# The value part of the row gradients, moved from the weight-gradient stage into the backward loop

## The chip, the cores and the metric

The kernel runs on one core of one Trainium2 chip. The metric is the device time in microseconds of one execution. A core has five engines that run side by side: TensorE (PE in the profile, with its weight loads as PEld), VectorE (DVE), ScalarE (ACT), GpSimd (POOL) and SyncE (SP). Each executes its own instructions in their order and waits on semaphores for the others. SP, ACT and POOL issue DMAs, which 16 DMA engines carry out. The DMAs that SP issues are the hardware queue q1 of the profile, POOL's are the software queue q0.

## The reference

The reference computes one forward pass and all its gradients (a vector-Jacobian product). Per 32-token segment, an attention over 8 memory rows and 32 token rows runs with 32 heads of 128 features, and its first 8 output rows are the next segment's memory; the result is gated by a feed-forward block:

```python
xn = layernorm(x)                       # 2048 tokens, 640 wide
for s in range(64):                     # segments
    h = concat([mem, xn[32*s:32*s+32]]) # 40 rows
    q, k, v = h @ Wq, h @ Wk, h @ Wv    # 32 heads of 128
    p = softmax(mask(q @ k.T * scale))
    o = (p @ v) @ Wo
    mem, out[s] = o[:8], o[8:]
g = silu(swiglu(xn, w1, w3, w2))
y = x + out * g
# outputs: y and the gradients of x, mem0, Wq, Wk, Wv, Wo, w1, w3, w2 for a given gradient of y
```

Backward, the segments run from the last to the first, because the gradient of a segment's memory rows is the gradient of the previous segment's outputs. For each row of h the gradient is the sum of three products: the gradients of v, k and q of that row (4096 wide each), times the transposed Wv, Wk and Wq. The gradient of v is P transposed times the gradient of o before Wo (here gO).

## The kernel before

The stages follow each other on one core: layer norm and the feed-forward pass, the forward recurrence, the backward loop (`phase4_Abwd`), the weight-gradient stage (`phase6_Awgrads`), the gradient of Wo (`phase6b_gWo`) and the backward feed-forward pass (`phase5_Bbwd_ln`). Within a stage, `in_order` fixes each engine's order to the one in which the program is written.

**The backward loop.** `chain(t, gap)` is one step, for segment t, from 63 down to 0. It multiplies the incoming gradient rows by the turned Wo (`packed_half`, L306: four groups of 32 columns of the array at once), turns the result to features (`packed_sel`, L314), forms the gradients of P and of the scores for the 8 memory rows (L1226, L1236 to L1244, `bd`, `gkv` at L1195), and adds up the gradient of the memory rows in one PSUM bank with `packed_out` (L325). `packed_out` takes 64 matmuls for each of Wv, Wk and Wq; each has 8 columns (the memory rows) in a group of 32, so 24 columns of each group are unused. L1262 forms the gradients of the 8 queries from the key rows `kr`. `fold_add` (L334, L336) adds the bank's halves on ACT and DVE, `fold_turn` (L352) turns the sum to features, and L1283 puts it into the input of step t-1. So each step starts when `fold_turn` of the step before has ended.

Between these parts, `gap` puts the work on the ordinary rows: units of three segments and four heads (`ld`, `turn`, `dprob`, `dsoft`, `gmem`), two or three units a step, for t from 62 to 4. In the gap G4 one more product on PE (L1430, `WARM`) writes a bank that nobody reads.

**Loads.** For step t-1, `loads` (VTD, PM, QM: L1151, L1153, L1156), `load_k` (L1162, L1167) and `load_xp` (L1174) are issued by SP in the middle of step t, together with the unit loads (L1307, L265, L1311), two stores of dS (L1273) and the store of the step's gO rows (L1215). The key rows have two buffers, `krbs`, which alternate from step to step; so have Qst and Pm.

**The weight-gradient stage.** It runs eight passes (qd), each over 22 units of four heads. Per unit: `s1` turns dS (L1588), `s2` forms the gradients of v, k and q for the unit's rows (L1598), `s3` turns these to features (L1630) into `ring`, and `s4` multiplies them by Wv, Wk and Wq and adds to `acc` (L1648, 12 matmuls for 128 rows and half of the width). At the end of a pass, `wg` forms four heads of the three weight gradients (L1667). `Fetch` issues the unit loads five units ahead on SP and POOL. The finished row gradients go to GXA.

Of the kernel before, what the change touches and what calls it, by code (L numbers as in the profile page):

```python
# [9 lines left out]
BF16 = mybir.dt.bfloat16  # L10
# [6 lines left out]
P = 128  # L17
# [23 lines left out]
class K:  # L41
# [109 lines left out]
    def setup_dram(self):  # L151
# [15 lines left out]
        self.GXA = mk("GXA", (S, D))  # L167
        self.HRO = mk("HRO", (self.NR, D))
# [93 lines left out]

    def load_x(self, dst, off, srcs, eng):
        for (a, b, src) in srcs:
            eng.dma_start(dst[off + a:off + b], src)  # L265
# [64 lines left out]
def fold_add(k, pm, pool, tag="fup"):  # L330

    fs = pool.tile([64, 320], BF16, name="fsum", tag="fsum")
    up = pool.tile([64, 320], F32, name="fup", tag=tag)
    k.nc.scalar.copy(up[:], pm[64:128, 0:320])  # L334
    for c in (0, 160):
        k.nc.vector.tensor_tensor(fs[:, c:c + 160], pm[0:64, c:c + 160], up[:, c:c + 160], ALU.add)  # L336
    return fs


def fold_store(eng, dst, fs):  # L340

    for b in range(2):
        eng.dma_start(dst[:, 320 * b:320 * b + 320], fs[32 * b:32 * b + 8, :])
# [211 lines left out]
def recurrence(k, W0, W4, Wv, Wk_, Wq, Wo, own, ps, banks):  # L555
    nc, tc = k.nc, k.tc
    D, DC, S, H, HD, T = k.D, k.DC, k.S, k.H, k.HD, k.T
    with tc.tile_pool(name="achain", bufs=1) as ch, \
# [39 lines left out]
        def chain(t, gap):  # L598
# [96 lines left out]
            fs = fold_add(k, pm, ch)  # L695
# [387 lines left out]
def phase4_Abwd(k, out2, W0, W4, WT, own, ps, banks):  # L1083
# [20 lines left out]
    with tc.tile_pool(name="gst", bufs=1) as st, tc.tile_pool(name="gchain", bufs=1) as ch, \  # L1104
# [10 lines left out]
        Qsts = [two(k0[:, c:c + 256]) for c in (3072, 3328)]  # L1115
# [4 lines left out]
        krbs = [st.tile([120, 2048], BF16, name="krb")[:], vt[0:120]]  # L1120
# [9 lines left out]
        WARM = dict(G4=1)  # L1130
# [16 lines left out]
        def loads(t):  # L1147
# [4 lines left out]
            Pm = ch.tile([P, 2, 40], BF16, name="gPm", tag="gPm", bufs=2)  # L1152
            nc.sync.dma_start(Pm[:], k.PM[t].rearrange("p (a c) -> p a c", a=2))  # L1153
            Qst = Qsts[t % 2]
            for a in range(2):
                nc.sync.dma_start(Qst[:, a, :], k.QM[t, :, a * 2048:(a + 1) * 2048])  # L1156
            ins[t] = vT, Pm, Qst

        def load_k(t):
            kr = krbs[t % 2][0:104]  # L1160
# [23 lines left out]
        def chain(t, gap):  # L1184
# [3 lines left out]
            vT, Pm, Qst = ins.pop(t)  # L1188
            xp = xps.pop(t)
            bdP, bdS = bds  # L1190
            bd(nc.gpsimd, bdP, Pm)
            def gkv(i, lh, rh):
                pk = bB[:, 256 * i:256 * i + 256].rearrange("p (a c) -> p a c", a=2)
                for a in range(2):
                    nc.tensor.matmul(pk[:, a, :], lh[:, a, :], rh[:, a].rearrange("p h m -> p (h m)"), start=True, stop=True)  # L1195
                g_ = ch.tile([P, H, 8], BF16, name="gkv", tag=f"gkv{i}")
                nc.vector.scalar_tensor_tensor(g_[:].rearrange("p (u h) m -> p u (h m)", h=4),  # L1197
                                               pk.rearrange("p a (u c) -> p (a u) c", c=32), k.scale if i == 0 else 1.0,
                                               xp[:, :, i, :], op0=ALU.mult, op1=ALU.add)
                return g_  # L1200

            sg = ch.tile([P, 1024], BF16, name="gstg", tag="gstg", bufs=1)
# [8 lines left out]
            gmT = ch.tile([P, 2, 8, 16], BF16, name="gmT", tag="gmT")  # L1211
# [3 lines left out]
            nc.sync.dma_start(k.GOS[t // 4, :, :, t % 4].rearrange("g r c -> (g r) c"), sg[:])  # L1215
            gap("W1")
            gOst = ch.tile([P, 2, P], BF16, name="gOst", tag="gOst")
# [3 lines left out]
            nc.vector.tensor_copy(gOst[:], pgo[:])  # L1221
# [6 lines left out]
            gvT = gkv(1, gOst, bdP)  # L1228
            dprob_m(1)
            dPT = ch.tile([40, 2, P], BF16, name="dPT", tag="dPT")  # L1230
            nc.scalar.copy(dPT[:], psd.rearrange("p a q h -> p a (q h)"))
            gap("G1")
            packed_out(k, pm, gvT, WvT, True, False, 0, 5)
# [3 lines left out]
            pr = ch.tile([P, 2, 40], F32, name="gpr", tag="gpr")  # L1237
            nc.vector.tensor_tensor(pr[:], ps2[:], Pm[:], ALU.mult)
            Dm = ch.tile([P, 2], F32, name="Dm", tag="Dm")
            nc.vector.tensor_reduce(Dm[:], pr[:], axis=AX.X, op=ALU.add)  # L1240
            u = ch.tile([P, 2, 40], F32, name="gu", tag="gpr")
            nc.vector.tensor_tensor(u[:], ps2[:], bc_last(Dm[:], 40), ALU.subtract)
            dS = ch.tile([P, 2, 40], BF16, name="dSm", tag="dSm", bufs=2)
            nc.vector.tensor_tensor(dS[:], u[:], Pm[:], ALU.mult)  # L1244
# [3 lines left out]
            packed_out(k, pm, gvT, WvT, False, False, 5, 16)  # L1248
            gkT = gkv(0, Qst, bdS)
            ps3 = bview(bC, 104, 1, P, bf=True)[:, 0]  # L1250
            for a in range(2):
                nc.tensor.transpose(ps3[64 * a:64 * a + 40, :], dS[:, a, :], k.ident[:], tile_position=(0, 64 * a))
            dST = ch.tile([104, 8, 16], BF16, name="dSTm", tag="dPT")
# [10 lines left out]
            gqT = ch.tile([P, H, 8], BF16, name="gqT", tag="gqT")  # L1264
            for a in range(2):
                nc.scalar.activation(gqT[:, 16 * a:16 * a + 16, :], pgq[a], ACT.Copy, scale=k.scale)
            if t > 0:
                load_k(t - 1)
                ride(t - 1)
            with nc.allow_non_contiguous_dma(reason="mem rows of dS"):  # L1270
# [7 lines left out]
            fs = fold_add(k, pm, ch, "gstg")  # L1278
            gap("G4")
            if t > 0:  # L1280
                pt = fold_turn(k, bC, fs)
                gap("G5")
                nc.vector.tensor_copy(goxs[(t - 1) % 2][:, :, 0:8], pt[:])  # L1283
            fold_store(nc.gpsimd, k.m_rows(k.GWO, t - 1) if t > 0 else out2f, fs)
            gap("G6")

# [71 lines left out]
        def gmem(tl, qd):  # L1358
# [8 lines left out]
            ks = fl.tile([P, ns, 2, 4, 8], F32, name="gks", tag="gks", bufs=2)  # L1367
# [25 lines left out]
        def gap_of(t):  # L1393
# [5 lines left out]
            def gap(g):  # L1399
# [19 lines left out]
                elif g == "G5":  # L1419
                    at(gmem_ld, t, 1)  # L1420
                elif g == "G6":
                    at(dsoft, t, 2)
                if t == 0 and g == "G1":
# [26 lines left out]
        def gx_work():  # L1450
# [5 lines left out]
            for i, (x0, w) in enumerate(blocks):  # L1456
                for cg in range(4):
                    sg = ch.tile([P, 1024], BF16, name="gstg", tag="gstg", bufs=1)[:] if cg % 2 == 0 else xs2
                    for b in range(2):
                        gx_block(k, gx[:, i % 2], sg, (bA, bB)[b], WoT, x0, w, cg, b, nc.scalar)  # L1460
# [12 lines left out]
        for i in range(len(pro) + 2):  # L1473
# [15 lines left out]
            if i == len(pro):  # L1489
                for _ in work:  # L1490
                    pass
                loads(T - 1)
                load_xp(T - 1)
# [5 lines left out]
        assert not later  # L1499
        in_order(k, start)  # L1500
# [3 lines left out]
class Fetch:  # L1504

    def __init__(self, k, W0):
# [4 lines left out]
        t = W0.tile([P, 5 * self.NB * 512 + 12 * k.D], BF16, name="land", tag="w0")  # L1511
# [5 lines left out]
        self.ws = [four(t[:, c + 4 * k.D * i:c + 4 * k.D * (i + 1)]) for i in range(3)]  # L1517
# [774 lines left out]
```

## Time and profile before

| | us |
|---|---|
| median of three runs (lowest, highest) | 4712.01 (4704.07, 4719.22) |
| the profiled execution's own time | 4684.61 |
| its span, first to last instruction | 4682.7 |
| PE busy, share of the span | 4466.5 (95%) |
| DVE, ACT, POOL busy | 2244.7, 1587.4, 2098.4 |
| forward stages and turn to backward | 0 to 1826 |
| backward loop, from the second step on | 1826 to about 2898 |
| weight-gradient stage | about 2900 to 4115 |
| gradient of Wo, backward feed-forward | 4115 to 4682.7 |

A row of a timeline gives start, length, engine, line, operation, output and input names, and a count where equal instructions follow each other; a bracket at its end names the idle time before it and what ended it. `x40` with 2.34 us means that 40 matmuls together took 2.34 us, pipelined: the single one's length is more than the distance to the next. Names of buffers are those of the tile they are cut from: `kT` holds many small buffers of the loop, `gor`, `vt` and `krb` are row buffers.

### The profile page before, as it was taken

Reading aid. Unit: us, or ns where it says so; the run is one execution under the profiler, and the core shown is the slowest. Engines: PE = TensorE matmul, PEld = TensorE weight load, DVE = VectorE, ACT = ScalarE, POOL = GpSimd, SP = SyncE. Lnnn points to the kernel's source line nnn. Section 1 sums busy time; section 2 is a strip of 40 time slices with the busy share of each in tenths; the row PEclk is TensorE's granted clock in tenths of the full one; section 3 lists DMA queues with packets and bytes.
Section 4 is the critical chain, followed back from the end, with each engine's and each line's share of the span. In section 5 each row is a group of like instructions: output and inputs, shape, how many; then the busy total and the mean of one; then the engine's idle time right before and its main releaser. Section 6 shows DMA issues by size and latency. Waiting matters only on the chain. (4 is left out here: it accounts for less than half of the span.)

```text
span 4682.7 us, 159785 instructions
## 1 busy us (share of the span) xinstructions
PE 4466.5 (95%) x64504; PEld 2821.1 (60%) x64504; DVE 2244.7 (48%) x7156; ACT 1587.4 (34%) x4360; POOL 2098.4 (45%) x3528
## 2 busy tenths in 40 slices
PE   8999999999999898999999998999999999999999
PEld 4544555555555555666666665676667666666675
DVE  8734666666666534555555553343224432311460
ACT  5432555555544433333333332232223322200000
POOL 6532555555555423455444444354335533311440
PEclk9999999999999998999999999999999999999999
DMA  8773566666655677777777775664345543579783
GB/s 269 236 252 119 175 178 178 179 179 179 180 168 167 167 181 230 211 225 207 215 211 209 208 209 154 144 163 132 110 116 158 147 129 107 170 223 207 159 181 100
DMA packets 976843, 834.77 MB, mean 178 GB/s; under 512 B 518890, under 2 KB 858286, under 8 KB 974144
## 3 DMA queue, kind: packets, MB, share of 16 engines
q1 hardware_dynamic: 763879, 547.92, 42.2%
q0 software_dynamic: 129952, 228.13, 16.4%
q10 hardware_dynamic: 82275, 48.52, 4.0%
q8 instruction: 509, 8.34, 0.8%
q14 instruction: 228, 1.87, 0.1%
HBM read 472.66 MB, written 310.33 MB: 167 GB/s over the span
## 5 line engine op out<-in xcount | busy, mean ns | idle before, releaser
L1667 PE MATMUL wg<-gr,hr 128*128 128x512 bf16 x2400 | 521.7, 379 | 0.0
L1648 PE MATMUL g<-land,ghacc 128*128 128x320 bf16 x3072 | 459.9, 300 | 0.8
L1667 PEld LDWEIGHTS <-hr 128*128 128x128 bf16 x2400 | 233.9, 98 | 278.9
L306 PEld LDWEIGHTS <-hx 128*32 128x32 bf16 x10240 | 246.8, 96 | 229.1 <-issue 14.6
L1648 PEld LDWEIGHTS <-ghacc 128*128 128x128 bf16 x3072 | 289.2, 98 | 104.2 <-ACT ghacc L92 2.2
L90 DVE CAST wgo<-wg 128x512 bf16<-128x512 f32 x72 | 49.8, 692 | 471.2 <-PE wg L1667 471.2
L90 DVE CAST stg<-bank 128x512 bf16<-128x512 f32 x256 | 177.1, 692 | 158.6 <-PE bank L306 154.5
L880 POOL DMA_DIRECT2D OR<-xv x163 | 89.8, 551 | 361.1 <-ACT xv L92 338.5
L1613 POOL DMA_DIRECT2D GSP<-grs x48 | 25.5, 542 | 473.1 <-ACT grs L1605 472.0
L92 ACT COPY ghacc<-t6g 128x768 bf16<-128x768 bf16 (+1 forms) x176 | 137.1, 779 | 293.8 <-PE t6g L1630 284.5
L1324 POOL DMA_DIRECT2D VTD<-gvT x176 | 129.4, 742 | 218.7 <-ACT gvT L1323 209.5
L325 PEld LDWEIGHTS <-gkv 128*8 128x8 bf16 x8192 | 177.6, 86 | 82.2 <-issue 4.1
L832 POOL TENSOR_TENSOR xP<-xP,xrz 120x480 bf16<-120x480 bf16 x163 | 161.1, 988 | 76.0 <-DVE xrz L831 46.6
L812 ACT ACTIVATE xP<-xsp,xnm 120x120 bf16<-120x120 f32 (+1 forms) x540 | 186.1, 372 | 26.0 <-DVE xnm L794 25.9
L1654 DVE TENSOR_TENSOR ghacc<-ghacc,g 128x320 f32<-128x320 f32 x192 | 93.6, 487 | 209.9 <-PE g L1648 209.9
L336 DVE TENSOR_TENSOR fsum<-bank,fup 64x160 bf16<-64x160 f32 x254 | 69.5, 311 | 258.5 <-ACT fup L334 255.2
L92 ACT CAST wgo<-wg 128x512 bf16<-128x512 f32 x48 | 28.1, 585 | 479.8 <-PE wg L1667 407.0
L1371 POOL DMA_DIRECT2D GXP<-gks x157 | 91.0, 580 | 189.5 <-ACT gks L1369 188.8
L325 PE MATMUL bank<-Wo,oTm 128*32 128x320 bf16 x4032 | 154.2, 307 | 18.4 <-DVE oTm L684 18.4
L325 PE MATMUL bank<-WkT,gkv 128*8 128x320 bf16 x4096 | 162.8, 299 | 4.2 <-issue 2.2
L325 PE MATMUL bank<-WvT,gkv 128*8 128x320 bf16 x4096 | 166.4, 305 | 0.5 <-DVE gkv L1197 0.5
L306 PE MATMUL bank<-Wq,hx 128*32 128x512 bf16 x2560 | 161.6, 381 | 0.0
(389 smaller groups left out, 10916.1 us busy)
## 6 DMA issues: line engine op xcount, KB each, us to landing
QVS<-stg SPq DMA_DIRECT2D x128, 256.0 KB
kT<-VTD SPq DMA_DIRECT2D x64, 320.0 KB
PR<-xP POOLq DMA_DIRECT2D x168, 120.0 KB, 3.1
VTD<-gvT POOLq DMA_DIRECT2D x168, 120.0 KB, 4.0
land<-DSR SPq DMA_DIRECT2D x168, 120.0 KB
land<-PR SPq DMA_DIRECT2D x168, 120.0 KB
OR<-xv POOLq DMA_DIRECT2D x163, 120.0 KB, 3.0
orr<-OR SPq DMA_DIRECT2D x14, 1280.0 KB
```

Source lines behind the costliest of these rows:

```text
L90: return nc.vector.tensor_copy(out, in_)
L92: return nc.scalar.copy(out, in_)
L306: k.nc.tensor.matmul(bank[32 * g:32 * g + 32, :], x[:, dc, :], W[:, dc, c0:c0 + 512], start=(dc == 0), stop=(dc == k.DC - 1), tile_positio ...
L325: k.nc.tensor.matmul(pm[p0:p0 + nq, 0:320], x[:, h, :], W[:, h, 320 * b:320 * b + 320], start=(first and i == 0), stop=(last and i == 15), ...
L812: nc.scalar.activation(Pb[0:n, j, 0:n], sp[0:n, j, :], ACT.Exp, bias=nmx[0:n, j:j + 1], scale=k.scale, accum_out=Z[0:n, j:j + 1])
L832: eng.tensor_tensor(Pb[0:n, :, 0:n], Pb[0:n, :, 0:n], bc_last(rz[0:n], n), ALU.mult)
L880: q.dma_start(k.OR[120 * tl:120 * tl + n, c0:c0 + 512], v[0:n])
L1324: nc.gpsimd.dma_start(k.VTD[tl][:, :, h0:h0 + 4, :], vTq[:])
L1371: (nc.sync if (tl, qd) in pro else nc.gpsimd).dma_start(k.GXP[tl, :, qd, 0:ns], ks[:].rearrange("p s i h m -> p s i (h m)"))
L1648: nc.tensor.matmul(pg[:], ring[:, i, j, r0:r0 + P], Ws[qd][i][:, j, 320 * h:320 * h + 320], start=(i == 0 and j == 0), stop=(i == 2 and j ...
L1654: nc.vector.tensor_tensor(a, a, pg[:], ALU.add)
L1667: nc.tensor.matmul(pw[:], hr[:, tl, dc * P:(dc + 1) * P], grs[i][:, tl, :], start=(tl == 0), stop=(tl == NF - 1))
```

## The change

The value part of the row gradients is computed in the backward loop, and the weight-gradient stage computes the key and query parts alone.

- The stationary operand of the value product in `packed_out` becomes `gv`, with 32 columns per head: columns 0 to 7 are the memory rows of segment t as before, columns 8 to 31 are the value gradients of 24 of the 32 token rows of segment t+1, formed in the step before. The matmuls stay 64.
- `ride_v` forms them: 32 products of 40 rows (gO rows `rows`, probabilities `prc`), which `load_g` brings with eight DMAs on SP. `ride_copies` moves them into `gv` and, for the remaining 8 rows, into `lv`. Each fourth step `extra` multiplies `lv` by the turned Wv (64 matmuls in the gap G3). `last_v` does what is left after step 0.
- The results go to the new DRAM tensors GXV (through `fold_store`) and GXL, which `extra_rows` copies into GXV.
- `load_g(t)` stands after `load_k(t-1)` and ahead of the dS stores; `ride_v(t)` stands between the gap G4 and `fold_turn`. One of the two row buffers holds `rows`; `kr` is always the other. Qst, Pm, dS and gks have one buffer; several small tiles share the tag `seq`; `sg`, `prc` and `up` share one tile. `load_q` is split from `loads` and stands after `gkv(0)`. The mask product for P is moved from the step's start to the end of the step before. `WARM` is empty.
- In the weight-gradient stage, `s3` turns two parts (one copy on ACT, one on DVE), `s4` has 8 matmuls, and in the first pass `acc` starts from GXV rows that `gv_ld` loads on POOL. The value weights are no longer loaded. `s2` still forms the value gradients' rows, which `wg` needs.

```diff
@@ phase4_Abwd
-        Qsts = [two(k0[:, c:c + 256]) for c in (3072, 3328)]
+        Qst = two(k0[:, 3072:3328])
+        Pm, dS = [two(k0[:, c:c + 80]) for c in (3584, 3664)]
-        krbs = [st.tile([120, 2048], BF16, name="krb")[:], vt[0:120]]
+        rows = st.tile([120, 2048], BF16, name="gor")[:]
+        krbs = [rows, vt[0:120]]
+        gs = st.tile([P, 1152], BF16, name="gs")
+        sg, prc = gs[:, 0:1024], gs[0:104, 640:1152].rearrange("p (h c) -> p h c", c=32)
+        lv = st.tile([P, H, 32], BF16, name="lv")
+        gv = st.tile([P, H, 32], BF16, name="gv")
-        WARM = dict(G4=1)
+        WARM = {}
+        def load_q(t):
+            for a in range(2):
+                nc.sync.dma_start(Qst[:, a, :], k.QM[t, :, a * 2048:(a + 1) * 2048])
+        def load_g(t):
+            tl, s = t // 3, t % 3
+            nx = k.geo(tl)[2]
+            for a in range(2):
+                r = rows[64 * a:64 * a + 40]
+                nc.sync.dma_start(r[0:8].rearrange("r (g c) -> r g c", g=2),
+                                  k.GOS[t // 4, 2 * a:2 * a + 2, 0:8, t % 4, :].rearrange("g r c -> r g c"))
+                src = k.g_rows(t, a)
+                nc.sync.dma_start(r[8:40].rearrange("r (g c) -> r g c", g=2) if len(src.shape) == 3 else r[8:40], src)
+                for (p0, p1, r0) in ((0, 8, nx + 8 * s), (8, 40, 32 * s)):
+                    nc.sync.dma_start(prc[64 * a + p0:64 * a + p1],
+                                      k.PR[tl][r0:r0 + p1 - p0, 16 * a:16 * a + 16, 32 * s:32 * s + 32])
+        def ride_v(t):
+            pvs = [ps.tile([P, 16, 32], F32, name="rpv", tag="x", bufs=5) for _ in range(2)]
+            for j in range(16):
+                for a in range(2):
+                    p0 = 64 * a
+                    nc.tensor.matmul(pvs[a][:, j, :], rows[p0:p0 + 40, j * P:(j + 1) * P], prc[p0:p0 + 40, j, :],
+                                     start=True, stop=True, tile_position=(p0, 0))
+            return pvs
+        def ride_copies(t, pvs):
+            for a in range(2):
+                nc.scalar.copy(gv[:, 16 * a:16 * a + 16, 8:32], pvs[a][:, :, 0:24])
+                nc.scalar.copy(lv[:, 16 * a:16 * a + 16, 8 * (t % 4):8 * (t % 4) + 8], pvs[a][:, :, 24:32])
+        def extra(m, bank):
+            packed_out(k, bank, lv, WvT, True, True)
+            fs = fold_add(k, bank, lf[:, 0:640].bitcast(F32), lf[:, 640:960])
+            for b in range(2):
+                nc.gpsimd.dma_start(k.GXL[32 * m:32 * m + 32, 320 * b:320 * b + 320], fs[32 * b:32 * b + 32, :])
+        def extra_rows(m0, m1):
+            nc.gpsimd.dma_start(k.GXV[:, :].rearrange("(t r) d -> t r d", r=32)[4 * m0:4 * m1, 24:32],
+                                k.GXL[:, :].rearrange("(t r) d -> t r d", r=8)[4 * m0:4 * m1])
-            kr = krbs[t % 2][0:104]
+            kr = krbs[1][0:104]
@@ chain
-            packed_out(k, pm, gvT, WvT, True, False, 0, 5)
+            packed_out(k, pm, gv, WvT, True, False, 0, 5)
             if t > 0:
                 load_k(t - 1)
                 ride(t - 1)
+            load_g(t)
             gap("G4")
+            pvs = ride_v(t)
             if t > 0:
                 pt = fold_turn(k, bC, fs)
+                bd(nc.gpsimd, bdP, Pm)
                 gap("G5")
                 nc.vector.tensor_copy(goxs[(t - 1) % 2][:, :, 0:8], pt[:])
+            ride_copies(t, pvs)
             fold_store(nc.gpsimd, k.m_rows(k.GWO, t - 1) if t > 0 else out2f, fs)
+            if t + 1 < T:
+                fold_store(nc.gpsimd, k.GXV[32 * t + 32:32 * t + 56, :], fs, 8)
+        def last_v():
+            packed_out(k, pm, gv, WvT, True, True)
+            fs = fold_add(k, pm, up, ch.tile([64, 320], BF16, name="fsum", tag="fsum"))
+            fold_store(nc.gpsimd, k.GXV[0:24, :], fs, 8)
+            extra(0, bB)
+            extra_rows(0, 1)
-            ks = fl.tile([P, ns, 2, 4, 8], F32, name="gks", tag="gks", bufs=2)
+            ks = fl.tile([P, ns, 2, 4, 8], F32, name="gks", tag="gks")
+                if g == "G3" and t % 4 == 3 and t < T - 1:
+                    extra((t + 1) // 4, ps.tile([P, 512], F32, name="exb", tag="x", bufs=5))
+                if g == "G5" and t == 1:
+                    extra_rows(1, T // 4)
@@ phase6_Awgrads
-        def s3(u, i0, i1):
+        def s3(u):
+            for i in range(2):
+                pt = pa.tile([P, 4, nx], BF16, name="t6g", tag=bank("x", 5, 3))
+                gr = st.pop(("g", u, i + 1))
+                k.copy(ring[:, i, :, a:a + nx], pt[:], eng='sv'[i])
+        def gv_ld(p):
+            for (w, r0, h) in parts[p] if p < NTL else ():
+                if h == 0:
+                    gvs[w] = io.tile([P, D], BF16, name="gxv", tag="gxv", bufs=4)
+                    nc.gpsimd.dma_start(gvs[w][:], k.GXV[P * w:P * w + P, :])
-            for i in range(3):
+            for i in range(2):
                 for j in range(4):
                     nc.tensor.matmul(pg[:], ring[:, i, j, r0:r0 + P], Ws[qd][i][:, j, 320 * h:320 * h + 320],
             if qd == 0:
-                nc.vector.tensor_copy(a, pg[:])
+                nc.vector.tensor_tensor(a, gvs[w][:, 320 * h:320 * h + 320], pg[:], ALU.add)
```

## The prediction

> **What bounds the kernel now.** I read the page first: PE busy 95%, PEclk almost everywhere 9. A busy share is an average over stages, so next came the busy times of the stages the change touches: the backward loop, the first pass of the weight-gradient stage, and the rest of that stage.
>
> ```profile
> 1826.00:2882.00 1056.00, 1008.08 (x23674) 661.91 (x23678) 553.56 (x2814) 346.07 (x1157) 502.84 (x914) 1.00 0.71 204
> 2900.00:3000.00 100.00, 89.12 (x984) 70.61 (x984) 44.50 (x101) 39.40 (x65) 68.60 (x124) 0.91 0.87 209
> 3000.00:4115.00 1115.00, 1108.99 (x9407) 713.03 (x9406) 366.62 (x787) 306.53 (x510) 471.01 (x846) 1.00 0.48 132
> ```
>
> Columns: stretch, length, busy time of PE, PEld, DVE, ACT, POOL, PE clock, DMA share, GB/s. The loop (about 63 steps of 17.0 us) has PE at 95%, but the DMA engines are busy 0.71 as well. After 3000 us PE is busy 99.5%: what is taken from PE there is time. The first pass has DMA at 0.87 (1.0 from 2920 to 2960 in 20 us windows) and PE at 89%: data bound it.
>
> Then one step of the loop, in order of time, on PE (start, length):
>
> ```profile
> 2424.86 2.34 PE L306 MATMUL bank<-WoT,hx 128*32 128x512 bf16 x40
> ...
> 2434.95 0.59 PE L1262 MATMUL bank<-dSTm,vt 40*128 40x8 bf16 x32
> ...
> 2437.50 2.35 PE L325 MATMUL bank<-WqT,gqT 128*8 128x320 bf16 x64
> ...
> 2440.06 0.38 PE L1430 MATMUL bank<-WqT,ident 128*128 128x512 bf16 x1
> 2440.72 0.78 PE L352 MATMUL bank<-sel,fsum 64*128 64x8 bf16 x6 [0.29 <-DVE fsum L336]
> ...
> 2441.89 2.34 PE L306 MATMUL bank<-WoT,hx 128*32 128x512 bf16 x40
> ```
>
> Counted from the step's start: query products (L1262) end at +10.7, query part of the output starts at +12.6 (64 matmuls, 2.3 us), the warm-up product at +15.2, the fold's turn (L352) at +15.9, the next step at +17.0. The same step on SP, which issues its DMAs in written order:
>
> ```profile
> 2432.28 1.33 SPq L1156 DMA_DIRECT2D kT<-QM  x2
> 2433.66 0.47 SPq L1162 DMA_DIRECT2D krb<-KS  x1
> 2434.18 0.33 SPq L1167 DMA_DIRECT2D krb<-KS  x1
> 2434.55 0.32 SPq L1162 DMA_DIRECT2D krb<-KS  x1
> 2434.92 0.53 SPq L1167 DMA_DIRECT2D krb<-KS  x1
> 2435.56 1.25 SPq L1273 DMA_DIRECT2D DSR<-dSm  x2
> 2437.11 0.57 SPq L1174 DMA_DIRECT2D xp<-GXP  x1
> ```
>
> The four key loads take 1.9 us and start at +8.8, before L1262 ends: they fill the other of two buffers. Issuing costs 0.3 to 0.65 us a piece. By lines and medians SP spends about 11 us of 17 on it (with 0.07 us between issues, 13).
>
> Last, the stage where work goes away:
>
> ```profile
> 3097.35 1.79 PE L1648 MATMUL g<-land,ghacc 128*128 128x320 bf16 x12
> 3098.98 0.34 PE L1630 MATMUL t6g<-ident,gr 96*128 96x96 bf16 x4
> 3099.15 0.61 PE L1598 MATMUL r6p<-land 120*128 120x128 bf16 x8
> ```
>
> Start to start, 12 products of L1648 take 1.63 us (0.136 each), four transposes of L1630 0.17 us (0.042 each).
>
> **What the Trainium skill says.** "TensorE: Matmul & The Clock Gate", Part 3: matmuls on separate column groups run together, so a group's unused columns cost nothing. The trace agrees: 64 packed products with 8 columns take 2.35 us (0.037 each). Part 1 there: after a window of 3.4 us with too little work PE runs at half clock. The trace agrees: between 2900 and 2910 us PE is busy 4.17 us and the clock is 0.54. "DMA: Bandwidth & Descriptors", Anatomy of one DMA: about 2.0 us fixed from issue to semaphore; the small DSR stores from POOL land in 1.8 to 5.7 us, median 3.1. Same page, Issuing engines are not separate DMA queues: issue time is "usually small relative to the DMA itself"; in this loop the trace says otherwise.
>
> **Part 1, taken from the weight-gradient stage.** One third of 3072 products: 1024 x 0.136 = 139 us. One third of the 2112 transposes: 704 x 0.042 = 30 us. Together 169 us, 21 per pass of eight. The first pass is bound by data and gains 16 loads of 160 KB (2.6 MB, 12 us at 217 GB/s) for 0.65 MB of weights saved: I take 0 there (bounds +10 to -10). In the other seven, loads must come faster; the unit part of a pass now moves data at 0.81 to 0.98 share in its first 30 us, so I leave 2 to 3 us a pass to waits: 7 x 18.6 = 130 us gained (90 to 150). The copies shrink (ACT 798 ns for 768 columns becomes a 384-column one like DVE's 354) and stay beside PE.
>
> **Part 2, added products in the loop.** The packed value product now carries 24 row columns in the same 64 instructions: 0, by the price above. The extra product for the last rows: 64 x 0.037 = 2.34 us in every fourth step. The 32 row products (40 rows, 32 columns) are like L1262: 0.53 us a step. The warm-up product goes: 0.22 us a step. On PE alone: 15 x 2.34 + 63 x 0.3 = 54 us, less what falls into the 0.3 to 0.9 us that PE waits for fsum: about 40. ACT gets four copies (about 1.5 us a step on an engine busy 33%), POOL two more stores (1.06 us, busy 48%): both hidden beside PE; without that cover 1.5 and 1.1 us a step. The moved mask product on POOL only needs Pm, loaded 8 us earlier. Buffers that become single (gks, Pm, dS, the scratch tag) are reused no sooner than their readers end in the chain's own order; gks must see its store land (3.7 us) within 4.2, which would cost ACT up to 1 us ahead of the gstg copy if the step kept its length.
>
> **Part 3, added loads, on the path.** One row buffer now holds gradient rows, so the key rows have a single buffer: load_k must wait for L1262 (+10.7) instead of starting at +8.8. Behind it in SP's order stand eight new loads, and the row products wait for all eight. They stand in PE's order ahead of the fold's turn, behind which waits the whole next step.
>
> - load_k: +10.7 to +12.6.
> - load_g: two memory-row loads (like L1162, 0.79 together), two row loads (0.33 each, median of L1167), four loads of probabilities in 64-byte pieces, priced like DSR (0.62 each), eight gaps of 0.07: 0.79 + 0.67 + 2.5 + 0.5 = 4.5. Last issue starts at +16.4.
> - Landing 2.0 us later (bounds 1.8 and 3.1): +18.4. Row products 0.55, then turn to next step 1.17: +20.1 instead of +17.0, so 3.1 us a step, x 63 = 195 us. The 40 us of part 2 vanish in this wait.
> - On SP the DSR stores, GXP and the next unit loads stand behind load_g and start 4.5 us later or more. GXP is then issued at about +18.5, lands by +20.5, and is needed 4.5 us into the next step, so it does not set the end; a unit's rows loaded there are needed 3 us into the next step, about when they land.
> - PE then idles from +15.2 to +18.4. That nearly fills a clock window, except in the 15 steps with the extra product. In 48 steps I add 0.9 us for work at half clock: 43 us. No row shows it; bounds 0 and 1.7 (a whole window lost).
> - SP's total becomes 13 + 4.5 = 17.5 of 20 us; I add 0.1 us a step, 7 us.
>
> Sum for the loop: +245 us (bounds +70 and +390: every issue at 0.3 and landing 1.8, or landing 3.1 with issues of 0.9 for the 512-piece loads and a full window lost). DMA engines have room: 1280 pieces and 160 rows of 2 KB add to a share of 0.71, spread over a longer step.
>
> **Part 4, the seam.** At step 0 the eight loads stand behind the prefetch of the next stage; then two packed products, two folds and three dependent stores before the first unit: +10 us (5 to 15), partly in PE's wait of 5.8 us at 2902.
>
> Sum: +245 - 130 + 10 = +125 us. From the profiled 4684.6 us that is 4810; the runs' median lies 27 above the profile, so 4712 + 125 = 4837.
>
> **The rivals.**
>
> - A (0.58): as above, 4837; its own range 4750 to 4940.
> - B (0.18), ends below 4698: the loads come in time. Priced: with every issue at 0.3 (lowest seen 0.27 to 0.32) load_k and load_g take 4.4 us, the last starts at +14.8, lands at +16.6; the step grows by 1.3 us, 82 us in all: 4712 + 82 + 10 - 130 = 4674. It decides at (130 - 10) / 63 = 1.9 us a step, an average issue of 0.43 us with its gap, against the 0.52 that I sum. For it: plain two-dimensional loads (xP<-PR) take 0.38. Against: every row with three-dimensional pieces (QM, GXP, DSR) takes 0.57 to 0.63.
> - C (0.14): SP or the 64-byte pieces become the bound, and unit loads come late too: a step of 22.7 us, 5.7 x 63 - 120 = +240, 4950. For it: SP's load above, and steps of 18.3 to 19.8 us that occur already near 2233 and 2251. Against: median steps keep to 17.03.
> - D (0.10): A, and the weight-gradient stage is held by its loads and keeps half the gain: 4900.
>
> **How the numbers follow.** Within 0.3% (4698 to 4726) can't be told from no change. Faster: B and a little of A, 0.18; same 0.05; slower 0.77. The range goes to 4670, B's working, and 4975, past C, leaving out the tails of both.
>
> **What would show it.** Right: the first row product waits for a DMA onto gor or gs, some 3 us a step; steps near 20 to 21 us; PE clock below 1 in the loop; the key loads on SP start only after L1262's counterpart; L1648's counterpart has 2048 products, the stage is about 130 us shorter, its first pass unchanged. Wrong: row products that follow at once, steps under 19 us, or a stage that shortens by 70 or by 170.

## The result and the profile after

The changed kernel takes 4964.1 us (median of four runs, 4955.4 to 4970.9), the kernel before 4708.0 in runs beside it (4695.1 to 4719.2). The ratio is 1.054, with an interval of 1.051 to 1.058: slower by 5.4%. The profiled execution has a span of 4953.6 us where the kernel before has 4682.7.

The 271 us between the two spans, by the starts of the loop's feature copy (L1276, before L1221, once a step) and of the weight products (L1751, before L1667):

| piece | before | after | difference |
|---|---|---|---|
| start to the first step's copy | 1810.5 | 1824.1 | +13.6 |
| 63 steps of the loop | 1075.7 | 1387.1 | +311.4 |
| last step, seam, first pass up to its weight products | 113.3 | 127.6 | +14.3 |
| from there to the start of the last weight product | 1113.2 | 1043.8 | -69.4 |
| the rest | 570.0 | 571.0 | +1.0 |

Stretches of the changed kernel, which answer to the three that the prediction shows: the loop, seam with first pass, and the rest of the weight-gradient stage. Columns as there: stretch, length, busy time of PE, PEld, DVE, ACT, POOL, PE clock, DMA share, GB/s.

```profile
1826.00:3205.00 1379.00, 1166.51 (x26858) 763.89 (x26861) 568.06 (x2855) 423.93 (x1429) 589.17 (x1077) 0.89 0.66 179
3205.00:3340.00 135.00, 103.88 (x1264) 75.51 (x1257) 48.79 (x121) 38.38 (x80) 92.87 (x166) 0.82 0.76 193
3340.00:4384.00 1044.00, 982.68 (x7884) 605.33 (x7883) 364.55 (x786) 262.36 (x510) 472.50 (x847) 0.99 0.53 137
```

PE is busy 85% of the loop instead of 95%, at a clock of 0.89. The last stage has PE at 94%, where it had 99.5%: it no longer bounds that stage alone. A step of the loop on PE (start, length; a bracket names idle time and what ended it):

```profile
2415.34 3.94 PE L314 MATMUL bank<-WoT,hx 128*32 128x512 bf16 x40
...
2427.04 0.58 PE L1318 MATMUL bank<-dSTm,vt 40*128 40x8 bf16 x32
...
2429.58 2.35 PE L333 MATMUL bank<-WqT,gqT 128*8 128x320 bf16 x64
2434.64 0.17 PE L1194 MATMUL rpv<-gs,gor 40*128 40x32 bf16 x1 [2.33 <-DMA DSR<-kT]
2435.72 0.59 PE L1194 MATMUL rpv<-gs,gor 40*128 40x32 bf16 x31 [0.91 <-DMA gs<-PR]
2436.15 0.62 PE L358 MATMUL bank<-sel,fsum 64*128 64x8 bf16 x6
```

PE waits ahead of the row products (L1194) in two pieces. The store named in the first bracket is the event that ended last by the profile; the row products read `gs` and `gor` alone. After such a wait the clock is low: the step shown follows a wait of 4.7 us, and its first 40 products, by Wo, take 3.94 us instead of 2.34, at a granted clock of 0.59; those of the next step take 4.46 us at 0.50. The median over the 64 steps is 3.99 us. So the query products (L1318) end 12.3 us after the step's start instead of 10.7. The same step on SP's queue:

```profile
2424.89 0.32 SPq L1169 DMA_DIRECT2D kT<-PM  x1
...
2427.65 0.30 SPq L1216 DMA_DIRECT2D vt<-KS  x1
...
2429.43 0.33 SPq L1181 DMA_DIRECT2D gor<-GOS  x1
...
2431.67 1.80 SPq L1186 DMA_DIRECT2D gs<-PR  x2
2433.51 1.24 SPq L1330 DMA_DIRECT2D DSR<-kT  x2
```

The key loads start at +12.3, when L1318 ends; the eight new loads follow at +14.1; the last are out at +18.1. The page's group of the row products gives their whole idle time on PE:

```profile
L1194 PE MATMUL rpv<-gs,gor 40*128 40x32 bf16 x2048 | 47.8, 178 | 196.8 <-DMA gs<-PR 161.5
```

196.8 us over 64 steps is 3.1 us a step.

### The profile page after: what moved, and what is told of

It reads as the page before. It is cut to its first block, busy times and chain, and to the rows that moved or that the text cites. A ratio compares the mean times of both kernels' runs of the same rounds, so it can differ in the third digit from the quotient of the medians.

```text
span 4953.6 us, 163919 instructions
## 1 busy us (share of the span) xinstructions
PE 4489.7 (91%) x65848; PEld 2805.6 (57%) x65848; DVE 2254.3 (46%) x7190; ACT 1616.1 (33%) x4633; POOL 2198.5 (44%) x3707
## 3 DMA queue, kind: packets, MB, share of 16 engines
q14 instruction: 240, 1.97, 0.1%
## 5 line engine op out<-in xcount | busy, mean ns | idle before, releaser
L1751 PE MATMUL wg<-gr,hr 128*128 128x512 bf16 x2400 | 521.7, 379 | 0.1
L314 PEld LDWEIGHTS <-hx 128*32 128x32 bf16 x10240 | 272.1, 105 | 286.0 <-issue 105.2
L1751 PEld LDWEIGHTS <-hr 128*128 128x128 bf16 x2400 | 233.9, 98 | 279.1 <-issue 0.3
L1730 PE MATMUL g<-land,ghacc 128*128 128x320 bf16 x2048 | 329.8, 307 | 1.9 <-DVE ghacc L1734 1.7
L314 PE MATMUL bank<-WoT,hx 128*32 128x512 bf16 x2560 | 248.7, 564 | 5.1 <-DVE hx L1342 1.2
L1730 PEld LDWEIGHTS <-ghacc 128*128 128x128 bf16 x2048 | 195.0, 100 | 68.9 <-issue 2.2
L1194 PE MATMUL rpv<-gs,gor 40*128 40x32 bf16 x2048 | 47.8, 178 | 196.8 <-DMA gs<-PR 161.5
L1438 ACT ACTIVATE gks<-gkp 128x96 f32<-128x96 f32 (+1 forms) x352 | 71.4, 264 | 392.6 <-PE gkp L1435 352.2
L819 ACT ACTIVATE xP<-xsp,xnm 120x120 bf16<-120x120 f32 (+1 forms) x540 | 186.6, 374 | 25.7 <-DVE xnm L801 25.6
L1673 PE MATMUL r6p<-land 120*128 120x128 bf16 (+1 forms) x1408 | 122.9, 225 | 63.9 <-DMA land<-QVS 22.9
L333 PE MATMUL bank<-WvT,gv 128*32 128x320 bf16 x4160 | 174.4, 312 | 1.4 <-ACT gv L1200 0.8
L92 ACT COPY ghacc<-t6g 128x384 bf16<-128x384 bf16 (+1 forms) x176 | 82.6, 469 | 266.8 <-PE t6g L1706 264.0
L333 PE MATMUL bank<-WkT,kT 128*8 128x320 bf16 x4096 | 162.2, 299 | 2.6 <-DVE kT L1253 1.8
```

Of the source, the lines that this page charges most:

```text
L92: return nc.scalar.copy(out, in_)
L314: k.nc.tensor.matmul(bank[32 * g:32 * g + 32, :], x[:, dc, :], W[:, dc, c0:c0 + 512], start=(dc == 0), stop=(dc == k.DC - 1), tile_positio ...
L333: k.nc.tensor.matmul(pm[p0:p0 + nq, 0:320], x[:, h, :], W[:, h, 320 * b:320 * b + 320], start=(first and i == 0), stop=(last and i == 15), ...
L819: nc.scalar.activation(Pb[0:n, j, 0:n], sp[0:n, j, :], ACT.Exp, bias=nmx[0:n, j:j + 1], scale=k.scale, accum_out=Z[0:n, j:j + 1])
L1673: nc.tensor.matmul(pr[:, j * P:(j + 1) * P], lh[0:n, j, :], rw[i][0:n, j * P:(j + 1) * P], start=True, stop=True)
L1730: nc.tensor.matmul(pg[:], ring[:, i, j, r0:r0 + P], Ws[qd][i][:, j, 320 * h:320 * h + 320], start=(i == 0 and j == 0), stop=(i == 1 and j ...
```

## The experiments

The step is the distance of the first and the last copy of L1276 (or its counterpart), divided by 63: 17.07 us before, 22.02 after. Steps and totals of experiments are of one run each, against 4694 to 4714 for the kernel before beside them; the four runs of the changed kernel spread over 15.6 us.

**First: is it the loads' place, the loads, or the products?**

The loads early:

```diff
                 loads(t - 1)
+            load_g(t)
             packed_out(k, pm, gv, WvT, False, False, 5, 16)
...
-            load_g(t)
```

> The eight loads of load_g are issued ahead of load_q and load_k instead of behind them; nothing else differs from the changed kernel. Theory (the place in SP's order is the cost): the row products find their data and follow at once, PE no longer idles, the clock stays full; a step is 17.1 us plus 0.5 for the extra products and 0.1, so 17.7 instead of 22.0, and the kernel takes 4964 - 63 x 4.3 = about 4690 us. Rival (SP's total issue time or the DMA engines set the step): the order does not matter, steps stay above 20 us and the kernel above 4840.

Measured: 4840.2 us, step 20.26. The rival holds. The place is worth 1.76 us of the 4.95 that a step grew.

The row loads left out (the x-gradient's value part is not computed; the products stay and work on what lies in their buffers):

```diff
+        nc.gpsimd.memset(gs[:], 0.0)
...
-            load_g(t)
```

> load_g is left out; the row products work on what lies in their buffers (cleared once), so the gradient of x is not computed rightly. The loop keeps all products, copies and stores. Theory: a step of 17.6 us, the kernel at about 4685 us, within 20 us of the run with the loads issued early. Rival (the loads cost by their traffic and issue time wherever they stand): this kernel is faster than the one with early loads by more than 60 us, 1 us a step.

Measured: 4726.7 us, step 18.29. So all of the change in the loop except the loads (products, copies, stores, single buffers) costs 1.22 us a step, against some 0.5 expected, and the loads 3.73. The loads still cost 1.97 a step in the early place. The clause on the difference to the early placement decides as well: it is 113 us, more than 60, so the loads cost wherever they stand. The stretch from 2000 to 2800 us, early loads above, no row loads below, shows how:

```profile
2000.00:2800.00 800.00, 722.30 (x16834) 479.82 (x16827) 363.73 (x1852) 274.70 (x922) 383.32 (x702) 0.92 0.74 200
2000.00:2800.00 800.00, 760.20 (x18892) 519.51 (x18884) 406.35 (x2073) 304.84 (x1034) 428.81 (x784) 0.99 0.72 202
```

By the length of a step, PE is busy 18.3 us and idle 2.0 with the early loads, 17.4 and 0.9 without. The products are the same, so some 0.9 of the 1.97 us is work at the lower clock of 0.92, and the rest is idle time of PE. Early loads do not leave the clock whole.

Only the four probability loads left out, from the late place (the x-gradient's value part is not computed; `gs` is cleared once here too):

```diff
-                for (p0, p1, r0) in ((0, 8, nx + 8 * s), (8, 40, 32 * s)):
-                    nc.sync.dma_start(prc[64 * a + p0:64 * a + p1],
-                                      k.PR[tl][r0:r0 + p1 - p0, 16 * a:16 * a + 16, 32 * s:32 * s + 32])
```

> Of load_g's eight loads only the four of probabilities (64-byte pieces) are left out, so the gradient of x is not computed rightly; the four loads of gradient rows stay in their place. Theory (issues stand in line): four issues of about 0.65 us fall away, a step is 22.0 - 2.6 - 0.3 = 19.1 us, the kernel at about 4780 us. Rival (64-byte pieces are slow to land): more than the issue time is saved, a step under 18.2 us and the kernel under 4730.

Measured: 4838.3 us, step 20.30. Neither number: half of the eight loads is 1.72 us, about half of what all eight cost.

Fourteen warm-up products of 512 columns in the gap before the row products:

```diff
-        WARM = {}
+        WARM = dict(G4=14)
```

> The changed kernel with 14 warm-up products (0.22 us each, 3.0 us) in the gap G4, ahead of the row products, where PE waits for the loads. Theory (a part of the longer step is PE at half clock after the wait): the query products end at +10.9 instead of +12.3, the step is about 20.7 us, the clock in the loop above 0.97, the kernel at about 4885 us. Rival (the clock does not matter, the loads' time is fixed otherwise): the step stays at 21.8 to 22.2 us or grows.

Measured: 4897.7 us, step 21.15, query products ending at +10.7 again; the clock between 2000 and 2800 us is 0.99 where the changed kernel has 0.90. The theory holds, with a smaller gain than its 20.7 us: the warm-up gives back 0.87 us a step, 55 us.

**Second: what do the loads cost when they are early?** The early placement left 20.26 us. Three candidates: that they are waited for, that 1280 pieces of 64 bytes load the DMA engines, or SP's queue itself.

The loads where the early placement has them, without row products and copies (the x-gradient's value part is left out):

```diff
-            pvs = ride_v(t)
...
-            ride_copies(t, pvs)
```

> The early placement with its eight loads a step, but no row products and no copies of them: nobody waits for the loads (the x-gradient's value part is left out). The products alone, without the loads, cost 1.2 us a step (18.3 against 17.1). Theory, the loads cost what they put on the queue and on the DMA engines, waited for or not: step 18.8 us or more, total 4750 or more. Rival, what costs is the row products' wait for their landing: step 17.6 or less, total 4675 or less.

Measured: 4874.9 us. One line's view of the copy, from its first to its last start:

```profile
L1277 DVE COPY kT<-bank x64: 290/291/293, 1827.2 to 3117.7; 128x256 bf16<-128x256 bf16 x64
```

(3117.7 - 1827.2) / 63 = 20.48 us a step: the theory. Loads that nobody waits for cost as much as loads that are waited for, and the row products and their copies add nothing beside them. The wait for their landing is not needed for the cost. What waits instead is seen in the view of waits, 2000 to 2800 us (total, times, longest):

```profile
PEld L1388 <- issue: 40.9, 16, 7.0
PE gvpt L1388 <- DMA kT<-QVS: 37.8, 14, 7.0
```

These are a unit's transposes in a gap; their loads stand behind the eight on SP. In the same stretch the kernel before has 0.3 us of this wait on QVS, the changed kernel none.

The same bytes in large pieces, in the early place (the x-gradient's value part is not computed):

```diff
-                    nc.sync.dma_start(prc[64 * a + p0:64 * a + p1],
-                                      k.PR[tl][r0:r0 + p1 - p0, 16 * a:16 * a + 16, 32 * s:32 * s + 32])
+                    nc.sync.dma_start(gs[64 * a + p0:64 * a + p1, 640:1152],
+                                      k.PR[tl][r0:r0 + p1 - p0, 16 * a:16 * a + 4, :].rearrange("r h c -> r (h c)"))
```

> The early placement (step 20.3 us), and the four probability loads of a step fetch the same bytes as pieces of 1024 bytes from the head of each row instead of 64-byte pieces: 80 pieces in place of 1280. The values are not the wanted ones, so the x-gradient is not computed; all the work is. Theory, the period follows what the step puts on the DMA engines (12.7 us of 16 engines' time in 17.1 us before, 15.0 in 20.3 with the early placement, 0.74 busy in both): 0.9 us of 64-byte pieces become 0.3, step 19.4 to 19.6, total 4790. Rival, only their place in SP's queue and the landing behind it count: 20.0 or more, 4820 or more.

Measured: 4853.7 us.

```profile
L1276 DVE COPY kT<-bank x64: 290/292/292, 1823.9 to 3106.2; 128x256 bf16<-128x256 bf16 x64
```

20.35 us a step: the rival. The DMA share between 2000 and 2800 us fell from 0.74 to 0.72 and the step stayed: the size of the pieces is not the cause. The test is a small one, because by these shares the edit took only some 0.3 of 15 us of DMA time from a step; the bytes of the eight loads stayed in all three early kernels.

SP's queue is the candidate that fits. Added up from the timeline of SP's queue between 2000 and 2800 us, in whole steps and in us a step: issuing, pauses under 0.15 between issues, and the longer pauses, in which SP waits for a buffer, a result or a landing. The last column is the mean step of the whole loop; in that stretch alone the steps of the three early kernels are 20.5 to 20.6.

| kernel | DMAs | issuing | pauses | waits | step |
|---|---|---|---|---|---|
| before | 22.9 | 12.6 | 1.4 | 3.1 | 17.1 |
| after | 30.9 | 15.3 | 1.7 | 4.9 | 22.0 |
| loads early | 31.0 | 15.3 | 2.0 | 3.2 | 20.3 |
| early, nobody waits | 30.8 | 15.2 | 2.0 | 3.5 | 20.5 |
| early, large pieces | 30.8 | 15.2 | 2.0 | 3.4 | 20.4 |
| no row loads | 23.0 | 12.5 | 1.4 | 4.4 | 18.3 |

Eight loads add 3.0 to 3.4 us of issues and pauses, some 0.4 each. With them early, SP waits as little as it did before, 3.2 to 3.5 us, and three kernels that differ in products or pieces but not in the queue have one step, 20.3 to 20.5. This fits a queue that sets the step, but does not prove it. Issues, pauses and waits add up to the step in every kernel, the one before included, where PE is the busy engine; and the kernel without the four probability loads, in the late place, also has 20.3 with a shorter queue. The two longest of the remaining waits, with the loads early: 41.3 us in 39 steps are the mask load (L1169) waiting for DVE to read the single Pm (L1298), and 26.0 the first row load waiting for the store of the gO rows that it reads back.

**Third: another queue.** The early loads issued by ACT instead of SP, and in a second kernel by POOL (`nc.gpsimd`); all three calls in `load_g` alike:

```diff
-                nc.sync.dma_start(r[0:8].rearrange("r (g c) -> r g c", g=2),
+                nc.scalar.dma_start(r[0:8].rearrange("r (g c) -> r g c", g=2),
```

> As the early placement of the eight row loads (step 20.3 us, 4840), but issued by ACT. Theory, SP's one queue in order is the cost (its own issues and its waits for a dump or for a freed buffer stand ahead of the loads, and the loads ahead of the key loads and the dump of score gradients): step 19.0 us or less, 4755 or less; the rest above 18.3 is ACT's own issuing. Rival, the traffic is the cost (some thousand pieces of 64 bytes on the DMA engines, whoever issues them): step 19.9 or more, 4815 or more.

Measured: 5023.9 us, step 23.01: the rival's side, but beyond it; the excess is not traffic, as the other queue shows below. On ACT's timeline:

```profile
2409.99 0.40 ACTq L1184 DMA_DIRECT2D gor<-GOS  x1
2416.76 0.63 ACTq L1186 DMA_DIRECT2D gs<-PR  x2
...
2419.88 0.27 ACT L1311 COPY dSTm<-bank 104x128 bf16<-104x128 bf16 x1 [10.40 <-DMA gor<-GOS]
```

ACT does nothing from 2410.4 to 2416.8, and the chain's copy stands behind its eight issues.

> The same eight loads at the same early place, issued by POOL (0.44 busy in the loop; eight issues at 0.57 us are 4.6 us of a step there). Theory of SP's queue: step 19.3 us or less, 4775 or less, POOL's block-diagonal work being delayed a little. Rival, traffic: step 19.9 or more, 4815 or more, as with ACT.

Measured: 4867.1 us, step 20.50. SP is relieved (13.6 us of issues and pauses, 7.0 of waits), but the step stays: the rival's number again. The view of ACT's waits, 2000 to 2800 us:

```profile
ACT gks L1438 <- DMA GXP<-gks: 134.5, 30, 8.7
```

With one gks buffer, ACT waits for a store that now stands behind the loads on POOL, 134.5 us in 39 steps; with the loads on SP this wait is not among ACT's longest six. So neither run frees the loop, and on each new queue a waiter stands behind the loads. The steps of both are also what the rival of traffic forecast, 19.9 or more. No run keeps the issues and takes the bytes away, so how the 1.97 us divide between SP's queue and the traffic of the loads stays open.

**Fourth: the weight-gradient stage.** The seven later unit parts (between two groups of weight products) take 74.2 us on average after (72.3 to 76.9), 84.1 before; without waits they would be 84.1 less the 21 worked out in the prediction, 63. The page has the 2048 products that were to be left:

```profile
L1730 PE MATMUL g<-land,ghacc 128*128 128x320 bf16 x2048 | 329.8, 307 | 1.9 <-DVE ghacc L1734 1.7
```

The waits from 3340 to 4320 us (total, times, longest) show PE held by unit loads, a few microseconds at most each time:

```profile
PEld L1663 <- DMA land<-DSR: 21.5, 20, 2.8
...
PEld L1673 <- DMA land<-QVS: 18.0, 30, 1.6
```

The first of the unit parts:

```profile
3404.50:3476.70 72.20, 64.26 (x766) 50.99 (x765) 44.03 (x99) 32.36 (x64) 59.92 (x108) 1.00 0.77 212
```

POOL is busy issuing DMAs for 59.9 of 72.2 us, 47.7 of them for 84 loads of memory rows; SP issues 53.2 us of it; data flows at 225 to 235 GB/s once the stretch is under way. A sixth landing buffer (both `NB`), and in the same run a second place for the prologue's gks:

```diff
-        self.k, self.NB = k, 5
+        self.k, self.NB = k, 6
...
             ks = fl.tile([P, ns, 2, 4, 8], F32, name="gks", tag="gks")
+            if (tl, qd) in pro and pro.index((tl, qd)) % 2:
+                ks = lv[:].rearrange("p h c -> p (h c)")[:, 0:128 * ns].bitcast(F32).rearrange("p (s i h m) -> p s i h m", s=ns, i=2, h=4)
```

> Two edits at places two milliseconds apart, read separately. (a) The weight-gradient stage gets a sixth landing buffer in the space that the value weights left. Data theory: its unit parts (74.2 us in the changed kernel, about 63 without any wait) are held by bytes, at 225 to 235 GB/s; one unit of 600 KB more is fetched under the weight-gradient part, 2.6 us of each of seven passes: unit parts near 71.6 us, 18 us in all. Rival, what is late is only the single load behind a freed buffer: the sixth buffer hides it and unit parts fall to 66 us or less, 55 us in all. (b) Every second row-gradient accumulator of the prologue uses the space of the extra value rows instead of the one buffer. If the single buffer caused the prologue's 14 us, the loop begins 12 to 14 us earlier; if not, within 3 us of the changed kernel's. Total 4930 with the data theory, 4895 with the rival.

Measured: 4943.3 us. (a) Unit parts 73.3 us, 0.9 less: neither number. (b) The first copy starts at 1814.1, 10 us earlier, and the waits of ACT for gks stores in the last 170 us ahead of the loop fall from 25.7 to 13.5 us (13.1 before). But kernels that keep the single buffer start anywhere from 1813.2 to 1827.2, so that its share of the 13.6 us is not shown.

The memory-row loads issued by ACT instead of POOL:

```diff
-            k.load_m(r, tl, nm, c0, c0 + 512, nc.gpsimd)
+            k.load_m(r, tl, nm, c0, c0 + 512, nc.scalar)
```

> The memory-row loads of the weight-gradient stage (4.4 DMAs a unit) are issued by ACT instead of POOL; the bytes stay. Rival, POOL's issuing (0.57 us each, 2.5 us of a unit's 3.5, POOL 0.9 busy there) holds the unit parts: they fall from 74.2 to 67 us or less, 50 us in all, total 4915. Data theory: unit parts stay within 1.5 us of 74.2 and the total within 15 us of 4964; ACT, 0.5 busy there, has room for 4.4 issues at 0.3 to 0.6 us.

Measured: 5196.8 us; unit parts 101 to 106.5. ACT was held up as in the loop, so the run decides nothing between the two:

```profile
ACT gr L1680 <- DMA land<-QVS: 178.3, 62, 7.2
ACT gr L1680 <- DMA land<-KS: 144.4, 29, 7.7
```

The probability tiles of a unit not loaded after the tenth unit (the value weights' gradient is not computed):

```diff
-        nc.sync.dma_start(Pr[0:n], k.PR[tl][:, h0:h0 + 4, :])
+        if u < 2 * self.NB:
+            nc.sync.dma_start(Pr[0:n], k.PR[tl][:, h0:h0 + 4, :])
```

> The changed kernel; in the weight-gradient stage the probability tile of a unit is loaded for the first ten units only and stale afterwards, so the value weights' gradient is not computed rightly; all products stay. Of 600 KB a unit 120 are gone, none of them issued by POOL. Theory, the unit parts are held by bytes (225 to 235 GB/s): they fall from 74.2 us to 68 or less, 45 us or more in all. Rival, POOL's issuing of the memory rows holds them: within 1.5 us of 74.2, total within 15 us of 4964.

Measured: 4912.7 us, unit parts 69.4 us on average (67.7 to 70.8).

```profile
3396.20:3465.20 69.00, 62.86 (x767) 50.91 (x766) 43.87 (x99) 32.15 (x64) 61.49 (x111) 1.00 0.67 184
```

4.8 us less: the rival, POOL alone, falls, and the theory's 68 is just missed. The edit takes 120 of 600 KB and also one of SP's five or so issues a unit, so bytes and SP's issuing stay unseparated. With the DMA share down to 0.67, POOL issues for 61.5 of the remaining 69 us.

**All that helped, together**: early loads, 14 warm-up products, the gks place, six buffers, each by its diff above; everything is computed.

> All edits that helped, together: the eight loads early, 14 warm-up products in the gap ahead of the row products, every second row-gradient accumulator of the prologue in the extra rows' space, six landing buffers; everything is computed. If the gains add (early 124 us, warm-up 53, accumulators 5 to 10, sixth buffer 7 of 4964): 4765 to 4785, still slower than before. Rival, with the clock whole the loads are late again and eat the warm-up's gain: 4815 or more.

Measured: 4896.6 us, step 21.06: the rival's side. The gains do not add. In a step on PE:

```profile
2399.77 3.18 PE L1505 MATMUL bank<-WqT,ident 128*128 128x512 bf16 x14
2402.89 0.19 PE L1194 MATMUL rpv<-gs,gor 40*128 40x32 bf16 x1
2403.50 0.55 PE L1194 MATMUL rpv<-gs,gor 40*128 40x32 bf16 x31 [0.43 <-DMA gs<-PR]
```

The loads are not late again, as the rival supposed: the row products wait 0.4 us here, and 0.9 us in all between 2000 and 2800 us (28.8 with early loads alone). In that stretch the clock rises from 0.92 to 0.98, but PE is busy 20.3 us a step instead of 18.3: the warm-up's 3.2 us stand on PE's own path and cost more than the clock gives back. No version that was run beats the kernel before.

## Why the prediction was right or wrong

The side, slower, held. So did the range, but only because it was drawn past rival C: 4964 lies outside A's own 4750 to 4940, and 11 us under the upper end. The forecast of 4837 was 127 us too low; by the spans, +271 instead of +125, it was 146 (the changed kernel's profile lies nearer to its median, 9 us, than the one of before, 27). The agreement of 4964 with rival C's 4950 is partly chance: the loop cost 66 us more than A says, seam, prologue and rest 19 more, and the weight-gradient stage gave 61 less, as D says it might.

- **Where PE waits** (A's core). Right: the row products stand still 3.1 us a step, predicted some 3, and the key loads start only after L1318. That the size agrees is partly luck, since the loads land later than predicted and PE comes later too.
- **The step's length.** Predicted 20.1 and 0.8 for clock and SP, measured 22.0. Three terms of its path were mis-sized (medians of the steps of the changed kernel). The loads start at +14.3, not +12.6: the half clock ahead delays L1318 by 1.6 us, and key loads and row loads with it. The prediction added the clock as a sum of its own, 43 us, and did not let it move the loads; the warm-up run gives 55 us for it. The issues were cheaper than priced: the probability loads take 0.32 us, not 0.62, and all eight are out 3.7 us after the first one starts, not 4.5. And the landing was slower: from the start of the last probability load to the second group of row products, which waits for it, pass 3.0 us (1.9 to 4.0), not 2.0. The prediction had this length in its own trace, as the median 3.1 of the small DSR stores, and used it as a bound only; the 2.0 us of the Trainium skill, "DMA: Bandwidth & Descriptors", Anatomy of one DMA, is for DMAs that POOL issues, and these are SP's.
- **SP's total.** This is the part of the mechanism that failed: "I add 0.1 us a step, 7 us". The prediction gave the eight loads almost no cost beyond their place on the path; taken off that place they still cost 1.97 us a step. The sum compared SP's issues, 17.5 us (measured 17.0), with a step of 20 and took the rest for free. SP's waits stand in the same order, 3.1 us a step in the trace of before; if they stay, the queue needs 20.1 to 20.5 with the loads, and the three early kernels have that step, whether the loads are waited for or not. That is the best account at hand, not a proof: the loads' traffic is not separated from it. In the changed kernel itself the queue has 4.9 us of waits and the path sets the step. Rival C put such a bound at 22.7 us for the changed kernel; its late unit loads appear only where the row loads are early. The Trainium skill's sentence in "DMA: Bandwidth & Descriptors", Issuing engines are not separate DMA queues, that issuing is usually small beside the transfer, speaks of one DMA and is not contradicted there: a probability load takes 0.32 us to issue and the last one 3.0 us to its use. It is the sum over 31 DMAs a step, 15.3 us of SP, that counts here.
- **Added products.** "The 40 us of part 2 vanish in this wait": with the loads gone they and the rest of the change cost 1.22 us a step, 77 us; with early loads nothing (20.26 with row products and copies, 20.48 without). So they do vanish as long as the loads are there. The packed value product itself stayed free: its 20 and 44 products take 0.86 and 1.68 us with 32 columns, 0.85 and 1.67 before with 8.
- **Single buffers.** Counted as free but for up to 1 us. Pm gives SP its longest wait; whether that lengthens the step was not tested. A share of gks in the prologue's 13.6 us is possible and not shown.
- **Part 1.** First pass: predicted 0, and with the seam +10; measured +14.3 together with the last step, inside the bounds. Later passes: -69 instead of -130. The prediction left 2 to 3 us a pass for late loads; it was 11 (74.2 against 63). POOL's 62 us of issuing in a unit part were to be read in the trace before: a part of 65 would have left it 3. Of which of POOL's issues, SP's issues and bytes the 11 us are made stays open; the run without probability tiles shows that POOL's issuing alone is not all.

In sum, by the runs: all but the loads +1.22, loads wherever they stand +1.97, their late place with the clock +1.76, together 4.95 us a step, 311 us, of which the other stage gave back 69.

## What to carry to other kernels

Price an added load twice: for its place ahead of its reader, and for what it does to everything else that shares its queue and the DMA engines. Here eight loads that nobody waited for made a step as long as loads that were waited for (20.5 and 20.3 us). An account of a queue by issues, pauses and waits shows how much room is left if the waits stay; it adds up to the step in any kernel, so which of them is the limit takes an experiment. When work is taken from the engine that bounds a stage, look up how long the next ones are busy there (here POOL, 62 of 84 us, and SP with 58 of issuing and short pauses) before counting the gain. Cures of two waits on one path do not add: the warm-up gained 66 us of the total alone and the early loads 124, and both together, with two more edits, 68.

## What the runs showed that was not expected

- Pieces of up to 64 bytes were a small burden: 11 ns each on a DMA engine in the run with early loads, against 55 for those of 512 to 1024 bytes, and 80 large pieces in place of 1280 of them a step changed nothing.
- The same probability loads take 0.32 us to issue on SP and 0.65 on POOL (medians).
- Issuing can stand still. At 2412 us in the run with loads on ACT, two loads of SP took 6.19 us to issue, while ACT paused for 6.4 between two of its own; the DMA engines were busy 0.98 to 0.99 from 2412 to 2416 at about 350 GB/s. That the full DMA engines held both back is likely and was not tested.
